# Weight words put together from end bytes, the first block moved behind the second pair, and later sums spread by transposes

## The chip, the cores and the metric

One core of one Trainium2 chip. The metric is device microseconds of one execution. The kernel before takes 706.54 us, the median of three runs (705.92 to 707.37).

## The reference

Sliding-window attention with sinks (batch 4, 8 heads, 768 positions, head size 64, 4 sink keys, a window of 128), and its output, 3072 tokens by 512, goes through a two-layer network of width 2048 whose hidden function is piecewise.

```python
scores = scale * np.matmul(q, k.transpose(0, 1, 3, 2))
scores = np.where(is_sink | in_window, scores, -1000000000.0)
a = np.exp(scores - np.max(scores, axis=-1, keepdims=True))
a = a / (np.sum(a, axis=-1, keepdims=True) + 1e-09)
x = np.matmul(a, v)                       # to (B * S, H * D)
h = x @ w_in
g = np.where(h >= 1, h, np.where(h <= -1, 0.0, (h + 1) ** 2 / 4))
out = g @ w_out
```

Everything is float32, except that the two weights arrive as float64; the kernel reads each as a pair of 32-bit words, `low` and `x` (the high one).

## The kernel before, in words

Work goes in eight chunks of 384 tokens (four batches, two halves of the sequence). Each chunk has attention for eight heads, which fills `xn`, and then the network on those tokens: `stage1` (h, L588) for j = 0 to 15, and `stage2` (the output, L607) two j behind. The network of a chunk is interleaved on TensorE with the attention of the next chunk by `spread`, which deals out steps by weights written beside them. TensorE's order is the program's own (`manual_schedule`); the other engines are ordered by the framework's planner, which simulates the program, save where `queue` chains instructions of one engine or `keep_in_program_order` pins one.

The matmuls take each float32 as two parts: a part rounded to the engine's format, and the rest. For a weight, the float64 words are first put together to a float32 pattern, which is then split. That is the decoding. A block is two rows of tiles of w_in or w_out, 128 partitions by 1024 numbers; there are 16 blocks (`weights(n)`, n even for w_in, odd for w_out). For each block VectorE does three steps into a tile `bits` and one more, and ScalarE one:

- L170: the high word shifted left by 3, with the top two bits cleared
- L176: sign and top exponent bit put in
- L179: the three top bits of the low word put in
- L180: ScalarE rounds this to the high part
- L183: VectorE subtracts that, which gives the rest

The float64 words are loaded into tiles of the pool `wpool` (L205, 1 MB each; the first four on SyncE's queue, the others on ScalarE's). This pool has eight buffers. The decoded w_out blocks take their buffers from the same pool and keep them, while decoded w_in blocks have tiles of their own. So late in the decoding few buffers are left for raw words. After L179 nothing reads the raw words any more. `fetch` loads ahead by up to two blocks, less at the end.

The first four pairs of heads and the scores of the fifth run in `first_pairs`, before any network work. For each pair: scores on TensorE (L441), peaks on VectorE (L452, with their order chained), exponentials on ScalarE (L457), the sums' reciprocals (L464, L465), then `pair_r` and `pair_av`. `pair_r` (L505) spreads the reciprocals over the head's 64 rows by six small matmuls against the identity; L507 copies them to `xn`, and L496 multiplies the attention's product by them. Blocks 0 to 3 are decoded in this loop, in pieces: a block's first two steps behind a pair's sums, its third between the next pair's peaks, its fourth behind these. The other 12 blocks are spread over the first chunk's network. Pairs 5 to 7 and then single heads (`attn_steps`, L283 onward) are the attention that runs beside it. `pair_steps` holds the weights of the later pairs' steps.

Of the kernel before, what the change touches and what calls it, by code (L numbers as in the profile page):

```python
# [10 lines left out]
I32 = mybir.dt.int32  # L11
# [38 lines left out]
def attn_ffn(ctx, tc, qk, qkp, vx, vs, par, w_in, w_out, out):  # L50
# [113 lines left out]
    def decode_parts(t, w, words, pin=False, on=False):  # L164

        low, x = words[..., 0], words[..., 1]
        high, rest = (t[:, :, 0], t[:, :, 1]) if len(t.shape) == 4 else (t[:, 0], t[:, 1])

        def shift():
            first = nc.vector.tensor_scalar(w, x, 3, 0x3FFFFFFF, op0=ALU.logical_shift_left, op1=ALU.bitwise_and)  # L170
            if pin:
                tc.keep_in_program_order(first)
            queue(first, on)

        def sign():
            queue(nc.vector.scalar_tensor_tensor(w, x, -0x40000000, w, op0=ALU.bitwise_and, op1=ALU.bitwise_or), on)  # L176

        def tail():
            queue(nc.vector.scalar_tensor_tensor(w, low, 29, w, op0=ALU.logical_shift_right, op1=ALU.bitwise_or), on)  # L179
            queue(nc.scalar.copy(high, w.bitcast(F32)), on)  # L180

        def rest_of():
            queue(nc.vector.tensor_tensor(rest, w.bitcast(F32), high.bitcast(F32), op=ALU.subtract), on)  # L183

        return shift, sign, tail, rest_of

    def decode(t, w, words, pin=False):
        for f in decode_parts(t, w, words, pin):
            f()
# [4 lines left out]
    def weights(n):  # L194
# [4 lines left out]
        def fetch():  # L199
            for k in range(n, min(n + min(AHEAD if n > 2 else 1, NP // 2 - n // 2 - 1) + 1, NP)):  # L200
# [6 lines left out]
        def parts(on):  # L207
# [7 lines left out]
            return decode_parts(t, dec.tile([P, 2, DM], I32, name=f"bits{n % 2}"), words, pin=not on, on=on)  # L215

        def f():
            fetch()
            for g in parts(False):
                g()  # L220

        if n < WFIRST:
# [237 lines left out]
    def pair_sums(m):  # L460
# [4 lines left out]
        queue(nc.vector.reciprocal(r, r), on)  # L465
        st["r", m] = r
# [31 lines left out]
    def pair_r(m):  # L498
# [4 lines left out]
        for i in range(CT):  # L503
            for a in range(2):
# [4 lines left out]
    def pair_steps(m):  # L509
# [7 lines left out]
        pv = [(0.65, lambda: pair_r(m - 1)), (1.2, lambda: pair_av(m - 1)())]  # L517
# [5 lines left out]
    def first_pairs():  # L523
# [4 lines left out]
        for m in range(H // 2 + 1):  # L528
# [12 lines left out]
            if 0 < m < H // 2:  # L541
                d[2]()
            pair_scores(m, 2)
            if m:
# [4 lines left out]
            if m < H // 2:  # L549
                wsteps[m][0]()  # L550
                d = wsteps[m][1]()
                d[0]()
                if m:
                    pair_av(m - 1)()
                d[1]()
# [98 lines left out]
    spn = [dec.tile([P, P], F32, name=f"spn{i}") for i in range(2)]  # L654
    for t in vq + spn:
# [166 lines left out]
```

## Time and profile before

| what | value |
|---|---|
| median of three runs | 706.54 us |
| the profiled execution | 705.98 us, span 704.3 us |
| PE busy | 681.5 us, 97% |
| DVE busy | 510.3 us, 72% |
| ACT busy | 489.5 us, 70% |
| POOL busy | 278.8 us, 40% |

The span is what the profile covers of the execution; 1.68 us lie around it. PE is TensorE's matmuls, PEld its weight loads, DVE VectorE, ACT ScalarE, POOL GpSimd. Busy shares are averages over stages that differ: the first 135 us, in which the weights are decoded, are not like the rest. A matmul's end is modelled, so PE can show as busy in a stretch in which it also waits.

### The profile page before, as it was taken

The page shows a single profiled execution, that of the slowest core. Times are in us where ns is not written, and L with a number is a line of the kernel's source. Part 1 is how long each engine was busy: PE and PEld are TensorE (multiplying, and loading weights), DVE is VectorE, ACT ScalarE, POOL GpSimd, SP SyncE. Part 2 cuts the span into 40 slices and gives each one's busy share as a digit, 9 for nine tenths or more (in the row PEclk, how much of TensorE's full clock was granted, in tenths as well). Part 3 has the DMA queues.
Part 4 walks back from the last instruction along what each step waited for, and adds up shares of the span by engine and source line. Part 5 has one row for each costly group of instructions (what it writes and reads, how often), then busy time and mean ns, then how long its engine had stood idle before and what let it go on. Part 6 is the DMA issues. An engine that isn't in the chain of part 4 may idle for free.

```text
span 704.3 us, 12263 instructions
## 1 busy us (share of the span) xinstructions
PE 681.5 (97%) x3889; PEld 604.6 (86%) x3889; DVE 510.3 (72%) x1405; ACT 489.5 (70%) x1241; POOL 278.8 (40%) x470
## 2 busy tenths in 40 slices
PE   5899998999999999999999999999999999999996
PEld 3567877899999999989889999899899999989995
DVE  7888998887776877688777878878787877642221
ACT  4886667687778868777787877777776876554332
POOL 3003344744443445355554455635544444300000
PEclk9899999999999999999999999999999999999999
DMA  7864533132244344254333443434322310001001
GB/s 232 291 216 156 190 99 135 49 107 60 63 148 124 102 127 129 68 174 128 92 113 105 147 130 124 126 118 133 122 59 62 102 50 22 3 1 45 1 1 49
DMA packets 45441, 73.98 MB, mean 105 GB/s; under 512 B 10744, under 2 KB 30008, under 8 KB 45368
## 3 DMA queue, kind: packets, MB, share of 16 engines
q1 hardware_dynamic: 42104, 60.53, 28.2%
q10 hardware_dynamic: 3264, 12.58, 4.8%
q8 instruction: 33, 0.54, 0.3%
q14 instruction: 40, 0.33, 0.1%
HBM read 66.80 MB, written 6.29 MB: 104 GB/s over the span
## 4 chain that ended last, share of the span: by engine, by line
PE 79%; DVE 9%; DMA 3%; ACT 3%; POOL 3%; issue 2%; SPq 0%; ACTq 0%; POOLq 0%; DVEq 0%
PE h_ps L588 33%; PE o_ps L607 32%; PE ps_a L283 4%; PE ps_a L390 4%; PE ps_a L344 2%; DVE bits L176 2%; DVE bits L179 1%; DMA w<-w_in 1%; POOL q_l L269 1%; PE ps_a L474 1%; DVE w L183 1%; DVE bits L170 1%; PE ps_a L493 1%; DVE p L304 1%; DVE g L597 1%
## 5 line engine op out<-in xcount | busy, mean ns | idle before, releaser
L588 PE MATMUL h_ps<-x,wi 128*128 128x384 f32 x1536 | 310.2, 340 | 0.0
L588 PEld LDWEIGHTS h_ps<-x,wi 128*128 128x128 f32 x1536 | 262.2, 188 | 8.7 <-issue 1.5
L607 PE MATMUL o_ps<-w,gh 128*128 128x512 f32 x768 | 244.0, 398 | 0.0
L607 PE MATMUL o_ps<-w,gl 128*128 128x512 f32 x384 | 151.1, 393 | 0.4 <-POOL gl L599 0.4
L607 PEld LDWEIGHTS o_ps<-w,gh 128*128 128x128 f32 x768 | 134.3, 188 | 16.9 <-issue 1.7
L597 DVE SCALAR_TENSOR_TENSOR g<-g,h_ps 128x384 f32<-128x384 f32 x128 | 70.3, 549 | 61.7 <-ACT g L596 60.6
L595 ACT ACTIVATE g<-h_ps,half 128x384 f32<-128x384 f32 x128 | 73.9, 578 | 52.7 <-PE h_ps L588 52.0
L269 POOL TENSOR_TENSOR q_l<-r,q_h 128x384 fp32r<-128x384 f32 x48 | 51.1, 1064 | 122.7 <-ACT q_h L268 116.1
L598 ACT CAST gh<-g 128x384 fp32r<-128x384 f32 x128 | 65.5, 512 | 46.1 <-DVE g L597 44.9
L290 ACT ACTIVATE p<-p,peak 128x260 f32<-128x260 f32 (+1 forms) x144 | 71.5, 496 | 23.0 <-DVE peak L287 22.4
L607 PEld LDWEIGHTS o_ps<-w,gl 128*128 128x128 f32 x384 | 72.0, 188 | 17.8 <-POOL gl L599 0.7
L599 DVE TENSOR_TENSOR gl<-g,gh 128x384 fp32r<-128x384 f32 x112 | 67.3, 601 | 23.5 <-ACT gh L598 22.6
L267 DVE TENSOR_TENSOR k_s<-k_r,k_s 64x524 fp32r<-64x524 f32 (+1 forms) x44 | 49.1, 1115 | 34.4 <-ACT k_s L265 34.3
L596 ACT ACTIVATE g<-g 128x384 f32<-128x384 f32 x128 | 67.0, 524 | 2.0
L287 DVE CUSTOM_DVE_ANT_0 p<-ps_a,m 128x260 f32<-128x260 f32 (+1 forms) x144 | 57.0, 407 | 14.7 <-PE ps_a L283 13.8
L358 POOL TENSOR_SCALAR_AFFINE_SELECT pt<-pt 128x384 fp32r<-128x384 f32 (+1 forms) x96 | 51.3, 535 | 22.6 <-DVE pt L349 19.5
L304 DVE CUSTOM_DVE_ANT_0 p<-p,stat 128x128 f32<-128x128 f32 x128 | 57.0, 489 | 0.2
L356 POOL TENSOR_SCALAR_AFFINE_SELECT pt<-pt 128x384 fp32r<-128x384 f32 (+1 forms) x96 | 49.9, 521 | 8.8 <-ACT pt L348 4.9
L599 POOL TENSOR_TENSOR gl<-g,gh 128x384 fp32r<-128x384 f32 x16 | 23.4, 1461 | 67.7 <-ACT gh L598 64.2
L390 PEld LDWEIGHTS ps_a<-pt,v_s 128*128 128x128 f32 x304 | 42.4, 190 | 1.8
L390 PE MATMUL ps_a<-pt,v_s 128*128 128x256 f32 (+1 forms) x304 | 41.9, 275 | 0.0
L283 PE MATMUL ps_a<-k_s,q_h 128*128 128x260 f32 (+1 forms) x144 | 40.7, 283 | 1.2 <-DVE sk L352 0.9
(151 smaller groups left out, 933.1 us busy)
## 6 DMA issues: line engine op xcount, KB each, us to landing
r<-qk SPq DMA_DIRECT2D x48, 192.0 KB
k_r<-qk SPq DMA_DIRECT2D x32, 262.0 KB
again<-w_in SPq DMA_DIRECT2D x16, 512.0 KB
again<-w_out SPq DMA_DIRECT2D x16, 512.0 KB
w<-w_in ACTq DMA_DIRECT2D x6, 1024.0 KB
w<-w_out ACTq DMA_DIRECT2D x6, 1024.0 KB
out<-o SPq DMA_DIRECT2D x23, 256.0 KB
r<-vx SPq DMA_DIRECT2D x32, 128.0 KB
```

The lines of the kernel that those rows point to most:

```text
L269: nc.gpsimd.tensor_tensor(q_l, q_r, q_h.bitcast(F32), op=ALU.subtract)
L283: nc.tensor.matmul(ps[:, lo:260], lhsT=q[:, i * P:(i + 1) * P], rhs=k_s[:, c0:c0 + 260 - lo], start=(j == 0), stop=(j == len(qs) - 1))
L290: nc.scalar.activation(p[:, i, lo:260], p[:, i, lo:260], AF.Exp, bias=peak_i, scale=-1.0, accum_out=stat[:, i:i + 1])
L304: nc.vector.tensor_tensor_reduce(out=own, in0=own, in1=p[:, i, 0:P], scale=r, scalar=0.0, op0=ALU.add, op1=ALU.add, accum_out=stat[:, i:i ...
L390: nc.tensor.matmul(z, lhsT=w, rhs=y, start=(n == 0), stop=(n == len(mms) - 1))
L588: nc.tensor.matmul(h_ps[:, :T], lhsT=w_i[j][:, w, ct * P:(ct + 1) * P], rhs=x[:, y, ct], start=(ct == 0 and n == 0), stop=(ct == NCT - 1 a ...
L595: nc.scalar.activation(g, h_ps[:, :T], AF.Relu, bias=half, scale=0.5)
L596: nc.scalar.activation(g, g, AF.Square)
L597: nc.vector.scalar_tensor_tensor(g, g, 1.0, h_ps[:, :T], op0=ALU.min, op1=ALU.max)
L598: nc.scalar.copy(gh, g)
L599: (nc.gpsimd if row0 == GL_POOL else nc.vector).tensor_tensor(gl, g, gh.bitcast(F32), op=ALU.subtract)
L607: nc.tensor.matmul(o_ps[tt], lhsT=gg[:, tt * P:(tt + 1) * P], rhs=w_o[j][:, w], start=(j == 0 and n == 0), stop=(j == NJ - 1 and n == 2))
```

## The change

The decoding has four VectorE steps as before, of other kinds. Two steps write single bytes into a tile `ends`, which GpSimd has set to zero once: byte 0 of each word gets the low word's top three bits, byte 3 gets the sign bit xor 0xC0. A third step shifts the high word left by 3 and xors it with `ends`. Its result goes over the low words in the raw tile, so every second word; only the last block's goes to `ends`. ScalarE's copy and the subtraction read it there. So a raw tile is in use until the subtraction. There is one `ends` tile in place of two `bits` tiles.

The prefetch depth is changed to `max(NP // 2 - 1 - (n + 1) // 2, 0)` instead of `NP // 2 - n // 2 - 1` (each at most two). Blocks 14 and 15 are loaded by a call behind block 13's and 14's steps.

In `first_pairs` all of block 0 comes behind the second pair's last peaks (pair index 1); blocks 1 to 3 have their first byte step behind the sums and the second behind L496.

For pairs 4 to 7 the reciprocal is written out to 128x384, each value 64 times, into a buffer of `q_l`. `pair_r` then does three 128x128 transposes of it instead of six matmuls, and its step weight for pairs 5 and on is 0.35 instead of 0.65.

```diff
--- before.py
+++ after.py
@@ -161,32 +161,43 @@
     with tc.issue_after(behind):
         nc.gpsimd.memset(both, -1)
 
-    def decode_parts(t, w, words, pin=False, on=False):
+    def decode(t, w, words):
 
         low, x = words[..., 0], words[..., 1]
         high, rest = (t[:, :, 0], t[:, :, 1]) if len(t.shape) == 4 else (t[:, 0], t[:, 1])
-
-        def shift():
-            first = nc.vector.tensor_scalar(w, x, 3, 0x3FFFFFFF, op0=ALU.logical_shift_left, op1=ALU.bitwise_and)
-            if pin:
-                tc.keep_in_program_order(first)
-            queue(first, on)
+        nc.vector.tensor_scalar(w, x, 3, 0x3FFFFFFF, op0=ALU.logical_shift_left, op1=ALU.bitwise_and)
+        nc.vector.scalar_tensor_tensor(w, x, -0x40000000, w, op0=ALU.bitwise_and, op1=ALU.bitwise_or)
+        nc.vector.scalar_tensor_tensor(w, low, 29, w, op0=ALU.logical_shift_right, op1=ALU.bitwise_or)
+        nc.scalar.copy(high, w.bitcast(F32))
+        nc.vector.tensor_tensor(rest, w.bitcast(F32), high.bitcast(F32), op=ALU.subtract)
+
+    def decode_parts(t, ends, words, w, on):
+
+        x = words[..., 1]
+        b = words.bitcast(U8).rearrange("p j c (w e) -> p j c w e", e=4)
+        e = ends.rearrange("p j c -> p (j c)").bitcast(U8).rearrange("p (j c e) -> p j c e", j=2, e=4)
+        high, rest = t[:, :, 0], t[:, :, 1]
+
+        def put(i):
+            if not on:
+                tc.keep_in_program_order(i)
+            queue(i, on)
+
+        def tail():
+            put(nc.vector.tensor_scalar(e[..., 0], b[..., 0, 3], 5, 0x07, op0=ALU.logical_shift_right,
+                                        op1=ALU.bitwise_and))
 
         def sign():
-            queue(nc.vector.scalar_tensor_tensor(w, x, -0x40000000, w, op0=ALU.bitwise_and, op1=ALU.bitwise_or), on)
-
-        def tail():
-            queue(nc.vector.scalar_tensor_tensor(w, low, 29, w, op0=ALU.logical_shift_right, op1=ALU.bitwise_or), on)
+            put(nc.vector.tensor_scalar(e[..., 3], b[..., 1, 3], 0x80, 0xC0, op0=ALU.bitwise_and, op1=ALU.bitwise_xor))
+
+        def word():
+            queue(nc.vector.scalar_tensor_tensor(w, x, 3, ends, op0=ALU.logical_shift_left, op1=ALU.bitwise_xor), on)
             queue(nc.scalar.copy(high, w.bitcast(F32)), on)
 
         def rest_of():
             queue(nc.vector.tensor_tensor(rest, w.bitcast(F32), high.bitcast(F32), op=ALU.subtract), on)
 
-        return shift, sign, tail, rest_of
-
-    def decode(t, w, words, pin=False):
-        for f in decode_parts(t, w, words, pin):
-            f()
+        return tail, sign, word, rest_of
 
     top = {}
     loaded = []
@@ -197,7 +208,7 @@
             return (w_in, w_out)[k % 2][k // 2 * 2:k // 2 * 2 + 2].bitcast(I32).rearrange("j p c -> p j c")
 
         def fetch():
-            for k in range(n, min(n + min(AHEAD if n > 2 else 1, NP // 2 - n // 2 - 1) + 1, NP)):
+            for k in range(n, min(n + min(AHEAD if n > 2 else 1, max(NP // 2 - 1 - (n + 1) // 2, 0)) + 1, NP)):
                 if k not in raw:
                     raw[k] = wpool.tile([P, 2, 2 * DM], I32, name="w")
 
@@ -212,13 +223,16 @@
                 w_o[j:j + 2] = t[:, 0], t[:, 1]
             else:
                 t = wi2[n // 2]
-            return decode_parts(t, dec.tile([P, 2, DM], I32, name=f"bits{n % 2}"), words, pin=not on, on=on)
+            return decode_parts(t, ends[n % len(ends)], words, ends[n % len(ends)] if n == NP - 1 else words[..., 0], on)
 
         def f():
             fetch()
             for g in parts(False):
                 g()
-
+            if NP - 4 < n < NP - 1:
+                wsteps[n + 1].load()
+
+        f.load = fetch
         if n < WFIRST:
             return fetch, lambda: parts(True)
         return f
@@ -462,8 +476,13 @@
         stat = st.pop(("sum", m))
         r = stat[:, :, CT:2 * CT]
         queue(nc.vector.tensor_scalar(r, stat[:, :, 0:CT], 1.0e-9, None, op0=ALU.add), on)
-        queue(nc.vector.reciprocal(r, r), on)
-        st["r", m] = r
+        if on:
+            queue(nc.vector.reciprocal(r, r))
+            st["r", m] = r
+        else:
+            wide = st["r", m] = att.tile([P, CT * P], F32R, name="q_l").bitcast(F32).rearrange(
+                "p (i a d) -> p i a d", a=2, d=D)
+            nc.vector.reciprocal(wide, r.rearrange("p a i -> p i a").unsqueeze(3).broadcast_to([P, CT, 2, D]))
 
     def early_transp(u, part):
 
@@ -501,6 +520,9 @@
         ps = ps_a.tile([P, 512], F32, name="ps_a")
         r = st.pop(("r", m))
         for i in range(CT):
+            if m >= H // 2:
+                nc.tensor.transpose(ps[:, i * P:(i + 1) * P], r[:, i].rearrange("p a d -> p (a d)"), ident)
+                continue
             for a in range(2):
                 nc.tensor.matmul(ps[a * D:a * D + D, i * P:(i + 1) * P], lhsT=r[:, a, i:i + 1].broadcast_to([P, D]),
                                  rhs=ident, start=True, stop=True)
@@ -514,7 +536,7 @@
         if m < NATIVE // 2:
             steps.append((0.0, lambda: pair_values(m)))
         tp = [(0.35, lambda u=u, i=i: early_transp(u, i)) for u in (a, b) for i in range(2)]
-        pv = [(0.65, lambda: pair_r(m - 1)), (1.2, lambda: pair_av(m - 1)())]
+        pv = [(0.35 if m > H // 2 else 0.65, lambda: pair_r(m - 1)), (1.2, lambda: pair_av(m - 1)())]
         dg = [(0.0, lambda: pair_sums(m))] if m < NATIVE // 2 else []
         if m % (H // 2) == 0:
             return steps + tp[:3] + sc[:1] + tp[3:] + pv[:1] + sc[1:2] + pv[1:] + sc[2:] + dg
@@ -538,21 +560,24 @@
                 pair_av(m - 1)()
             pair_scores(m, 0)
             pair_scores(m, 1)
-            if 0 < m < H // 2:
+            if 1 < m < H // 2:
                 d[2]()
             pair_scores(m, 2)
-            if m:
+            if m == 1:
+                for f in wsteps[0][1]():
+                    f()
+            elif m:
                 d[3]()
             if 0 < m < H // 2:
                 pair_r(m - 1)
             pair_sums(m)
             if m < H // 2:
                 wsteps[m][0]()
-                d = wsteps[m][1]()
-                d[0]()
                 if m:
+                    d = wsteps[m][1]()
+                    d[0]()
                     pair_av(m - 1)()
-                d[1]()
+                    d[1]()
 
 
     chunks = [(b, t) for t in (0, CT) for b in range(B)]
@@ -652,6 +677,10 @@
     dec = early.enter_context(tc.tile_pool(name="dec", bufs=1))
     vq = [dec.tile([P, CT + 1, 2, D], F32, name=f"vq{i}") for i in range(2)]
     spn = [dec.tile([P, P], F32, name=f"spn{i}") for i in range(2)]
+    ends = [dec.tile([P, 2, DM], I32, name=f"ends{i}") for i in range(1)]
+    with tc.issue_after(behind):
+        for t in ends:
+            nc.gpsimd.memset(t, 0)
     for t in vq + spn:
         nc.vector.memset(t, 0.0)
     p0 = [att.tile([P, CT, 260], F32, name="p").rearrange("p i c -> p (i c)") for _ in range(2)]
```

## Rows read from the trace of the kernel before

**Rows 1.** Busy time by stretch: length, then PE, PEld, DVE, ACT, POOL; clock, DMA.

```profile
13.00:43.00 30.00, 22.89 (x193) 15.76 (x190) 27.68 (x77) 23.79 (x77) 0.91 (x2) 0.89 0.77 257
43.00:70.00 27.00, 27.00 (x166) 21.83 (x166) 23.10 (x43) 18.98 (x50) 6.97 (x5) 1.00 0.49 174
70.00:105.00 35.00, 35.00 (x216) 27.46 (x215) 32.85 (x50) 22.40 (x55) 14.85 (x10) 1.00 0.44 145
105.00:135.00 30.00, 27.43 (x156) 22.64 (x155) 26.02 (x50) 20.29 (x51) 17.65 (x17) 1.00 0.29 103
140.00:170.00 30.00, 30.00 (x172) 27.42 (x171) 24.33 (x78) 23.27 (x64) 15.49 (x30) 1.00 0.30 89
```

**Rows 2.** Chain of waits from 70 to 105 us, its shares by engine and line.

```profile
by line: DVE bits L176 21.6%; DVE bits L179 16.1%; issue 10.1%; DVE w L183 10.0%; DVE wi L183 8.7%; DVE bits L170 7.7%; DVE g L597 7.3%; DVE pt L452 4.0%; DVE p L452 3.2%; ACT wi L180 3.1%; DVE stat L464 2.6%; PE ps_a L441 2.0%; ACT pt L457
```

**Rows 3.** The decoding lines: count, duration ns min/median/max, first and last start, form.

```profile
L170 DVE TENSOR_SCALAR bits<-w x16: 650/682/1046, 12.9 to 123.8; 128x1024 int32<-128x1024 int32 x16
L176 DVE SCALAR_TENSOR_TENSOR bits<-w,bits x16: 1210/1225/2074, 13.6 to 124.9; 128x1024 int32<-128x1024 int32 x16
L179 DVE SCALAR_TENSOR_TENSOR bits<-w,bits x16: 1209/1224/1925, 15.9 to 129.7; 128x1024 int32<-128x1024 int32 x16
L180 ACT CAST w<-bits x8: 1046/1048/1052, 25.7 to 130.9; 128x1024 fp32r<-128x1024 f32 x8
L183 DVE TENSOR_TENSOR w<-bits,w x8: 1217/1224/1225, 26.7 to 132.0; 128x1024 fp32r<-128x1024 f32 x8
```

**Rows 4.** Timeline of DVE, first pairs: start us, us, instruction, idle before it.

```profile
12.88 0.70 DVE L170 TENSOR_SCALAR bits<-w 128x1024 int32<-128x1024 int32 x1 [2.91 <-DMA w<-w_in]
...
14.76 0.28 DVE L452 CUSTOM_DVE_ANT_0 pt<-o_ps,m 128x128 f32<-128x128 f32 x1
...
22.51 0.29 DVE L452 CUSTOM_DVE_ANT_0 p<-o_ps,m 128x128 f32<-128x128 f32 x1 [0.61 <-PE o_ps L441]
```

**Rows 5.** Timeline of PE, first pairs.

```profile
11.12 1.23 PE L441 MATMUL o_ps<-k_s,q_h 64*128 64x128 f32 x5
...
19.59 0.44 PE L474 MATMUL ps_a<-ident,pt 128*128 128x128 f32 x2 [1.13 <-ACT xn L507]
...
42.72 0.77 PE L588 MATMUL h_ps<-x,wi 128*128 128x384 f32 x3
```

**Rows 6.** The reciprocals by line, columns as in Rows 3.

```profile
L296 DVE RECIPROCAL stat<-stat x48: 165/176/179, 122.3 to 602.5; 128x3 f32<-128x3 f32 x48
L465 DVE RECIPROCAL stat<-stat x8: 183/190/192, 9.8 to 106.5; 128x6 f32<-128x6 f32 x8
```

**Rows 7.** Chain of waits in order of time: start us, us on the chain, what.

```profile
62.69 0.33 PE ps_a L474 x3
...
107.90 0.81 PE ps_a L505 x12
```

**Rows 8.** Last weight blocks: timelines of ACT's queue and DVE; one stretch as Rows 1.

```profile
103.81 0.38 ACTq L205 DMA_DIRECT2D w<-w_in  x1
117.20 0.38 ACTq L205 DMA_DIRECT2D w<-w_out  x1
...
118.40:121.80 3.40, 2.54 (x14) 1.94 (x13) 2.46 (x9) 3.40 (x14) 2.17 (x2) 1.00 0.77 308
...
111.59 1.23 DVE L183 TENSOR_TENSOR w<-bits,w 128x1024 fp32r<-128x1024 f32 x1 [0.65 <-ACT w L180]
123.76 0.68 DVE L170 TENSOR_SCALAR bits<-w 128x1024 int32<-128x1024 int32 x1
131.99 1.23 DVE L183 TENSOR_TENSOR w<-bits,w 128x1024 fp32r<-128x1024 f32 x1 [0.65 <-ACT w L180]
```

**Rows 9.** Timelines of PE and of its weight loads around the last block.

```profile
124.29 2.25 PE L588 MATMUL h_ps<-x,wi 128*128 128x384 f32 x12
...
133.27 0.19 PEld L607 LDWEIGHTS o_ps<-w,gh 128*128 128x128 f32 x1 [0.36 <-DVE w L183]
134.13 0.19 PEld L607 LDWEIGHTS o_ps<-w,gl 128*128 128x128 f32 x1 [0.68 <-POOL gl L599]
```

## The prediction

> **What bounds the kernel now.** I read busy time by stretch first. After 140 us TensorE has no gap and the other engines have room, so only what happens before that can move the end, and a shift there is kept to the end [rows 1]. From 13 to 43 us VectorE is busy 27.68 of 30.00. From 43 to 70 it has 3.9 us free and TensorE none. From 70 to 105 it is busy 32.85 of 35.00 [rows 1]. TensorE shows as full there too, but its weight loads have fallen from 0.91 of the time (27.42 of 30.00, after 140) to 0.78 (27.46 of 35.00), so part of that is waiting [rows 1]. The chain of waits says whose work it waits for: from 70 to 105 it runs through VectorE, the decoding lines above all [rows 2]. The decoding ends late: TensorE waits at 133.27 for the subtraction of the last weight block, then until 134.13 for another operand [rows 9]. So there are three places to watch: VectorE before 43, VectorE from 70 to 113, and the arrival of blocks 14 and 15.
>
> **The decoding steps.** A block costs VectorE 0.682 + 1.225 + 1.224 + 1.224 = 4.36 us by the medians [rows 3]. The change takes out L170, L176 and L179 and adds two byte steps and one shift-and-xor. No row shows a byte step on VectorE. The bounds come from the two kinds of step over the same 1024 numbers: 0.68 (L170, one source) and 1.22 (L176, two sources) [rows 3]. A byte step has one source and takes every second word, as L170 does, so I take 0.68. The shift-and-xor is L176's kind, 1.22, but writes every second word. L170 and L176 already read that way, and L176 is no slower than L183, which reads without gaps [rows 3]. Writing that way isn't in the trace; nearest is again 1.22, and 1.9 is what L176 and L179 reach when disturbed (their maxima are 2.07 and 1.93) [rows 3]. I take 1.22. New sum: 2 x 0.68 + 2 x 1.22 = 3.81, so 0.54 less per block. ScalarE's copy (1.05) and L183 now read spaced words; I leave them as they are for the same reason.
>
> [...]
>
> **The first block.** VectorE sits idle for 2.91 us until the words of block 0 arrive at 12.88. It then spends 1.88 us on them before the second pair's first peak at 14.76, though the scores of that pair were begun on TensorE at 11.12 [rows 4, 5]. With the block behind the peaks they can start soon after 11.12, nearly 3 us earlier (I leave 0.8 us for the first matmul and its hand-over). The block's load stays where it is. Not all of the gain stays. The block's subtraction now follows its third step directly, so VectorE stands idle for ScalarE's copy (1.05). The next pair is also held by a loop in which VectorE has no part: its transposes wait for the copy of the spread sums on ScalarE (19.59), and its first peak waits for TensorE (22.51) [rows 4, 5]. Three microseconds less one, and blocks 1 to 3 at 0.54 less each as far as that loop lets them through: 1.1 to 2.4. I take 1.8 for the start of the network, now at 42.72 [rows 5].
>
> **The spread sums.** Six matmuls took 0.81 on the chain for a pair, three 128x128 transposes take 0.33 [rows 7]: 0.48 less, four times, on TensorE where it is full. The price is on VectorE: a reciprocal of 384 instead of 6 per partition. The trace has 3 and 6 per partition: medians 176 and 190 ns, so 4.7 ns a number and 0.16 fixed [rows 6]. That makes 0.16 + 384 x 4.7 ns = 1.95, or 1.8 more than now. From the ends of the two ranges, (183 - 179)/3 = 1.3 ns gives 0.7 and (192 - 165)/3 = 9 ns gives 3.6 [rows 6]; these are the bounds. All four lie between 43 and 107 us, where the decoding is, the last at 106.5 [rows 6].
>
> **The last loads.** Now a raw tile is free after a block's third step. After the change it is in use until the fourth, and with seven decoded w_out blocks in eight buffers block 14 can be loaded only when block 13 is through, and block 15 only when block 14 is. Before, block 14's load was issued at 103.81, nine microseconds before block 13's last step ended at 111.59 + 1.23 = 112.82 [rows 8]. So the new loads stand in one line with the decoding. One load: issued at 117.20, its 1.05 MB (3.4 us at 308 GB/s) over at 121.80 [rows 8], so 4.6 us. The loads before these get shallower too, but have some microseconds to spare. SyncE's queue is passed by none of this; the issue itself stands in ScalarE's queue, 0.38 each as before. GpSimd's one memset of `ends` is hidden: GpSimd is busy 0.91 of the 30 us after 13 [rows 1]. The wide reciprocals borrow the two buffers of `q_l`, so the first single heads' q_l come later; their GpSimd work only moves within the stretch.
>
> **The sum**, as shifts against the profiled execution:
> - At 43: 1.8 early.
> - 43 to 70: four blocks -2.2, two reciprocals +3.6, so VectorE +1.4, covered by its 3.9 free [rows 1]. Still 1.8.
> - 70 to 105: the blocks follow each other every (123.8 - 12.9)/15 = 7.4 us [rows 3], so five: -2.7, with one reciprocal +1.8. Now 2.7 early. TensorE's own saving lies beneath this.
> - Block 13's end: 112.82 - 2.7 + 1.8 (fourth reciprocal) - 0.54 = 111.4.
> - Block 14: load 4.6, own steps 3.81 + 1.05, and 0.8 for other work queued between: in hand at 121.7. TensorE needs it at 124.29 - 2.7 = 121.6 [rows 9]: just in time.
> - Block 15: 4.6 + 5.7 again: 132.0, against 133.22 before (131.99 + 1.23) [rows 8].
> - TensorE goes on at 132.1 instead of 134.13 [rows 9], since the other operand comes from block 14's matmuls and those are 2.6 early: 2.0 gained.
>
> The profiled execution took 705.98, so 704.0. The median of the runs lies 0.56 above it: 704.5. The 0.8 is the softest term; block 15 before took 9.46 from first to last step (123.76 to 133.22) for 5.40 of its own, so it can be 0 to 4 [rows 8]. If the loads are never last, the TensorE side gives 2.7 + 0.5, so 703.3, and with cheap reciprocals (0.7) some 701.5. I take 701.5 to 705.1 as this case's own range.
>
> **Rivals.**
> - *The late loads take everything.* A wait for data replaces the wait for VectorE: a byte step pinned in program order stands at the head of VectorE's queue until block 14's words land, and behind it wait the peaks and the g of the network, for which TensorE waits; the same holds on ScalarE if the load's issue, which waits for the buffer, is put ahead of ready work. Two microseconds instead of 0.8 around each of the two blocks make 2.4 more: 706.9. For it: 9.46 against 5.40. Against it: VectorE has little else to do there, 26.02 of 30.00 with the decoding itself in it [rows 1].
> - *The long reciprocal costs more, and it is slower.* Beyond 1.95, each extra microsecond counts twice (the third and the fourth; the first two have 2.5 left of the free time). From 3.0 us per reciprocal the gain is gone. At the bound, 3.6: 2 x 1.65 + 0.8 = 4.1 lost, 708.6. For it: the spread of so few rows; against it: the medians.
> - *Byte steps or the spaced write don't run at L170's rate, and it is slower.* From 0.13 more per byte step, or 0.26 for the write, the gain is gone. At 1.22 per byte step a block costs 1.08 more than I have: 43 to 70 4.3 less 2.5, then 5.4, then three more blocks 3.2: 10.4 lost, 714.9. Against it: L170.
>
> [...]
>
> **How the numbers follow.** Forecast 0.46; late loads 0.27; reciprocal 0.14; byte steps and write 0.13. A difference under 0.2% (1.4 us) can't be told from none, so the bound lies at 705.1 and 708.0. Faster 0.46, same 0.27, slower 0.27. The range takes in the first three cases and leaves out most of the last: 701.5 to 710.
>
> **What would show it.** Byte steps at 0.68 and the third step at 1.22 on the chip; the reciprocal of 384 near 1.95; the second pair's first peak near 12; the first network matmul near 41; ScalarE's two last loads right behind the subtractions of blocks 13 and 14; TensorE's wait near 132 for block 15. It is wrong if the third step or a byte step is dearer, if VectorE stands idle at 111 to 116 while TensorE waits for g, or if TensorE waits nowhere and the gain is over 3.

## The result, and the profile after

The changed kernel takes 716.21 us (median, 715.45 to 716.38); the kernel before, run beside it, 706.27. The ratio is 1.0136, with a 95% interval of 1.0118 to 1.0153: slower by about 9.7 us, where 2 us faster was forecast. The range ended at 710.0. The profiled execution took 716.11 us; its span is 714.3.

The stretches of after, to be read against [rows 1] (columns as there; the last one, 135 to 150, is not in [rows 1] and has its line of before beneath it):

```profile
13.00:43.00 30.00, 23.28 (x172) 15.72 (x172) 22.16 (x59) 20.24 (x65) 0.91 (x2) 0.77 0.70 232
43.00:70.00 27.00, 25.57 (x157) 20.38 (x154) 25.63 (x48) 19.82 (x53) 5.47 (x4) 1.00 0.58 201
70.00:105.00 35.00, 35.00 (x205) 27.87 (x204) 32.14 (x56) 22.71 (x57) 9.31 (x7) 1.00 0.32 108
105.00:135.00 30.00, 24.73 (x132) 20.83 (x131) 24.15 (x48) 18.45 (x47) 18.63 (x19) 0.89 0.44 145
135.00:150.00 15.00, 12.64 (x62) 10.91 (x61) 10.50 (x24) 8.48 (x23) 7.33 (x9) 0.89 0.13 34
...
135.00:150.00 15.00, 15.00 (x90) 13.95 (x89) 11.05 (x36) 12.39 (x35) 7.24 (x13) 1.00 0.34 106
```

Two stretches stand out. From 13 to 43 VectorE is busy 22.16 us instead of 27.68: it stands, with more work still to do. From 105 on TensorE has gaps, and its granted clock falls to 0.89. The first output block is sent at 151.24 instead of 142.62, 8.6 us later, and the lag is still there late in the program: an output block is sent at 565.18 in after and at 555.47 in before. From the network's start to the first output it is 105.3 us instead of 99.9, so about 3 us are lost ahead of the network and 5.4 in its first chunk.

Prices first: the lines that took the place of [rows 3] and [rows 6], columns as there.

```profile
L187 DVE TENSOR_SCALAR ends<-w x16: 698/766/1411, 14.0 to 134.5; 128x1024 uint8<-128x1024 uint8 x16
L191 DVE TENSOR_SCALAR ends<-w x16: 740/756/1577, 14.6 to 135.2; 128x1024 uint8<-128x1024 uint8 x16
L194 DVE SCALAR_TENSOR_TENSOR w<-w,ends x15: 1212/1226/2039, 15.4 to 125.0; 128x1024 int32<-128x1024 int32 x15
L195 ACT CAST w<-w x7: 1091/1131/1147, 28.4 to 114.8; 128x1024 fp32r<-128x1024 f32 x7
L485 DVE RECIPROCAL q_l<-stat x4: 2553/2553/2554, 47.8 to 107.5; 128x384 f32<-128x384 f32 x4
```

The byte steps cost 0.77 and 0.76 us, the step that writes every second word 1.23, ScalarE's copy 1.13 instead of 1.05, the wide reciprocal 2.55. So a block has become cheaper on VectorE, by 0.37 us where 0.54 was forecast, and each of the four reciprocals dearer by 2.36.

Now the head. ScalarE's timeline of after, with the idle time before an instruction in brackets:

```profile
21.95 0.30 ACT L340 CAST vsx<-vs_r 120x128 fp32r<-120x128 f32 x1 [2.59 <-DMA vs_r<-vs]
...
26.39 0.30 ACT L340 CAST vsx<-vs_r 120x128 fp32r<-120x128 f32 x1 [2.94 <-DMA vs_r<-vs]
```

In before the same two copies stood in the head without a wait:

```profile
22.27 0.29 ACT L326 CAST vsx<-vs_r 120x128 fp32r<-120x128 f32 x1
...
25.20 0.28 ACT L326 CAST vsx<-vs_r 120x128 fp32r<-120x128 f32 x1
```

They belong to the sink values of the first single heads, which are used after 110 us. The change does not touch them, but in the order that the planner now makes they stand further ahead: the second one, which stood behind four exponentials of the third pair, now stands before the first. ScalarE begins nothing else in these 2.59 and 2.94 us, so the pairs' own work stands behind a load that is not in. VectorE and TensorE wait with it:

```profile
23.49 0.56 DVE L644 TENSOR_TENSOR x<-xn,x 128x384 fp32r<-128x384 f32 x1 [1.10 <-ACT x L643]
...
29.49 1.22 DVE L198 TENSOR_TENSOR w<-w 128x1024 fp32r<-128x1024 f32 x1 [3.27 <-ACT w L195]
```

```profile
45.93 0.77 PE L613 MATMUL h_ps<-x,wi 128*128 128x384 f32 x3
```

The network starts at 45.93, 3.2 us later than in before and not 1.8 earlier. Last, the two late blocks; ScalarE's queue, VectorE and TensorE of after:

```profile
117.25 0.37 ACTq L216 DMA_DIRECT2D w<-w_in  x1
129.58 0.37 ACTq L216 DMA_DIRECT2D w<-w_out  x1
```

```profile
122.20 0.92 DVE L187 TENSOR_SCALAR ends<-w 128x1024 uint8<-128x1024 uint8 x1 [1.78 <-DMA w<-w_in]
123.02 1.56 DVE L191 TENSOR_SCALAR ends<-w 128x1024 uint8<-128x1024 uint8 x1
124.48 0.27 DVE L301 CUSTOM_DVE_ANT_0 p<-ps_a,m 128x128 f32<-128x128 f32 x1
```

```profile
127.38 1.08 PE L358 MATMUL ps_a<-ident,p 128*128 128x128 f32 x3 [4.62 <-DVE p L316]
129.54 3.22 PE L613 MATMUL h_ps<-x,wi 128*128 128x384 f32 x12
...
140.65 0.50 PE L632 MATMUL o_ps<-w,gh 128*128 128x512 f32 x1 [1.49 <-ACT w L195]
142.02 0.79 PE L632 MATMUL o_ps<-w,gh 128*128 128x512 f32 x1 [0.87 <-DVE w L198]
```

Block 14's load is issued at 117.25 instead of 103.81 [rows 8], directly behind block 13's last step. VectorE stands before the byte step at 122.20 with peaks of the single heads behind it (124.48), and TensorE stands 4.62 us. Before stood there too, but for 1.94:

```profile
122.89 0.87 PE L344 MATMUL ps_a<-ident,p 128*128 128x128 f32 x3 [1.94 <-DVE p L302]
```

After the longer gap the twelve matmuls of [rows 9] take 3.22 us instead of 2.25; the granted clock from 127 to 132 us is 0.54. Block 15 follows in the same way; TensorE goes on at 142 instead of 134.13.

### The profile page after: what moved, and what is told of

Its sections match the earlier page's. It is cut to its first block, busy times and chain, and to the rows that moved or that the text cites. A ratio compares the mean times of both kernels' runs of the same rounds, so it can differ in the third digit from the quotient of the medians.

```text
span 714.3 us, 12204 instructions
## 1 busy us (share of the span) xinstructions
PE 684.1 (96%) x3853; PEld 607.9 (85%) x3853; DVE 511.5 (72%) x1405; ACT 489.2 (68%) x1241; POOL 275.6 (39%) x471
## 5 line engine op out<-in xcount | busy, mean ns | idle before, releaser
L372 POOL TENSOR_SCALAR_AFFINE_SELECT pt<-pt 128x384 fp32r<-128x384 f32 (+1 forms) x96 | 49.2, 513 | 22.3 <-DVE pt L363 19.2
L370 POOL TENSOR_SCALAR_AFFINE_SELECT pt<-pt 128x384 fp32r<-128x384 f32 (+1 forms) x96 | 49.5, 516 | 8.4 <-ACT pt L362 4.3
L624 POOL TENSOR_TENSOR gl<-g,gh 128x384 fp32r<-128x384 f32 x16 | 21.2, 1327 | 74.0 <-ACT gh L623 68.1
```

The source lines that it names most:

```text
L624: (nc.gpsimd if row0 == GL_POOL else nc.vector).tensor_tensor(gl, g, gh.bitcast(F32), op=ALU.subtract)
```

## Experiments

Three suspects: **A**, ScalarE's queue in the head; **B**, the loads of blocks 14 and 15; **C**, the wide reciprocal. The first four runs take them out of the kernel after; then each part of the change is put into the kernel before by itself; the rest rebuild it. Ratios are against the kernel before, run beside each group of them on the same chip (medians 704.7 to 706.0). Letters e to h are four such groups; a difference between two groups is known to about 0.3 points.

| run | what | median us | ratio, 95% interval | first network matmul | first output |
|---|---|---|---|---|---|
| e1 | after, sink copies out of the head | 713.47 | 1.0124 (1.0089 to 1.0159) | 42.25 | 148.59 |
| e2 | after, word in its own tile, old loads | 710.00 | 1.0087 (1.0052 to 1.0121) | 46.8 | 145.67 |
| e3 | after, narrow reciprocal | 709.43 | 1.0069 (1.0039 to 1.0098) | 46.0 | 145.68 |
| e4 | after, all three | 704.83 | 1.0004 (0.9988 to 1.0020) | 43.33 | 141.84 |
| f1 | after, byte steps not pinned | 715.10 | 1.0123 (1.0095 to 1.0152) | 47.1 | 151.44 |
| f2 | before + moved first block | 711.68 | 1.0084 (1.0056 to 1.0112) | 43.11 | 144.25 |
| f3 | before + wide reciprocal, transposes | 710.17 | 1.0060 (1.0039 to 1.0081) | 41.1 | 144.16 |
| f4 | before + byte decode | 704.08 | 0.9971 (0.9950 to 0.9992) | 41.33 | 139.89 |
| g1 | f4 with word in raw tile, late loads | 706.06 | 1.0003 (0.9985 to 1.0020) | 41.0 | 140.76 |
| g2 | f4, sink copies out of the head | 703.03 | 0.9965 (0.9946 to 0.9983) | 39.6 | 138.17 |
| g3 | f4, first block behind four peaks | 707.84 | 1.0036 (1.0014 to 1.0057) | 44.40 | 142.94 |
| g4 | f4, sums spread by a copy | 703.00 | 0.9955 (0.9939 to 0.9971) | 41.2 | 136.98 |
| h1 | g2 and g4 together, first block moved | 703.77 | 0.9981 (0.9964 to 0.9999) | 42.78 | 139.18 |
| h2 | g2 and g4 together | 701.58 | 0.9950 (0.9932 to 0.9968) | 39.79 | 135.72 |

The last two columns are us in each run's profiled execution (before: 42.72 and 142.62; after: 45.93 and 151.24). Two things in these columns vary from one execution to the next. From the first output to the end it is 563.4 us in before and 563.4 to 565.9 in the others, so a difference of 2 us there says nothing. And with the first block in its old place the start depends on when that block's words land. f3 has the head of before unchanged, and there VectorE begins with them at 11.18, not at 12.88 as in [rows 4]:

```profile
11.18 0.69 DVE L170 TENSOR_SCALAR bits<-w 128x1024 int32<-128x1024 int32 x1 [1.21 <-DMA w<-w_in]
```

This is why its network starts at 41.1. In f4, g1 and g4 the words are waited for until 11.74 to 11.84, in g2 and h2 they are in by 11.4. So before's profile caught a late arrival, and 42.72 is some 1 to 1.7 us late as a yardstick.

**e1: the sink copies behind the head's last ScalarE instruction.**

```diff
-            nc.scalar.copy(vs_s[0:120], vs_r)
+            queue(nc.scalar.copy(vs_s[0:120], vs_r))
```

> The kernel after, with the two copies of the single heads' sink values (CAST vsx) put in ScalarE's queue behind the head's last ScalarE instruction. Theory head-queue (ScalarE stands 2.59 and 2.94 us before these copies for their load, and the whole head stands behind ScalarE): the first network matmul, at 45.93, comes at 41 to 43, and the time falls by 3 us, to about 713, less what the late loads take back. Rival (the head is late because of the order of block 0's own steps and the clock that fell): it stays within 0.7 us of 45.9 and the time within 0.7 us of 716.2. Rival late-loads (all of the loss is made at 110 to 145): the first network matmul moves, the time does not.

The network starts 3.7 us earlier, so theory A is right about the head: the waits were ScalarE's. But of the 3.7 us the first output keeps 2.65, and the ratio falls by only 0.12 points, well inside its interval. The late loads wait for block 13, whose last step came 3.5 us earlier too (112.5 for 116.0), and TensorE's stall is the same:

```profile
123.82 1.08 PE L358 MATMUL ps_a<-ident,p 128*128 128x128 f32 x3 [4.59 <-DVE p L316]
```

What a gain at 42 us is worth at the end could not be told in time from this run.

**e2: the word in a tile of its own, and the loads of before.** Theory B's test.

```diff
-            return decode_parts(t, ends[n % len(ends)], words, ends[n % len(ends)] if n == NP - 1 else words[..., 0], on)
+            return decode_parts(t, ends[0], words, dec.tile([P, 2, DM], I32, name="bits"), on)
-            ... max(NP // 2 - 1 - (n + 1) // 2, 0)) ...
+            ... NP // 2 - n // 2 - 1) ...
-            if NP - 4 < n < NP - 1:
-                wsteps[n + 1].load()
```

> The kernel after, with the word of each block in a tile of its own, so that the raw words' tile is free at the third step, and with the loads asked for where they were before. Theory late-loads (word kept in the raw tile makes the loads of blocks 14 and 15 wait for the blocks before; then VectorE stands at a byte step with peaks behind it): block 14 is in hand before 115, block 15 ends at 134 to 136 for 141.96, the time falls by 4 to 6 us, to 710 to 712. Theory head-queue alone: the first network matmul stays at 45.9 and everything after is set by it, time falls by under 1.5 us. Theory wide reciprocal: under 1.5 us.

The load of block 14 is issued at 106.63 instead of 117.25, TensorE's stall is 2.31 us, block 15 ends at 134.9. The ratio falls by 0.49 points, about 3.5 us: less than 4 to 6, more than the rivals allow. Block 14 came at 122.5 and not before 115: VectorE was still behind, its third step done only at 120.1. The edit also gives ScalarE's copy unspaced words again (1.05 us for 1.13), so it is not of the loads alone; g1 below settles how much that counts.

**e3: reciprocals of six numbers and six matmuls again.** Theory C's test.

```diff
+        queue(nc.vector.reciprocal(r, r), on)
+        st["r", m] = r
...
-            nc.vector.reciprocal(wide, r.rearrange("p a i -> p i a").unsqueeze(3).broadcast_to([P, CT, 2, D]))
...
-                nc.tensor.transpose(ps[:, i * P:(i + 1) * P], r[:, i].rearrange("p a d -> p (a d)"), ident)
```

> The kernel after, with the reciprocals of the later pairs back at six numbers a partition and the sums spread by six matmuls each. Theory wide reciprocal (2.55 us on VectorE four times, 2.36 us more than the narrow one each, of which VectorE's queue passes on most): the sum of block ends between 46 and 122 gains 2 to 4 us and the time falls by 2 to 4 us. Rivals head-queue and late-loads: VectorE catches up in between, the time falls by under 1 us, since blocks 14 and 15 wait for their loads and not for VectorE's time; with the loads as the bound it is 9.4 us of VectorE's time that cost nothing.

The ratio falls by 0.67 points, 4.7 us, more than theory C gave it. The network starts as late as in after, yet block 13 ends at 113.7 instead of 117.2, with it the late loads come earlier, and the stall shrinks to 2.46 us. So the reciprocals and the late loads act on the same chain.

**e4: the three edits together.**

> All three of these edits together in the kernel after; what stays of the change is the byte decode (3.81 for 4.36 us of VectorE a block) and the moved first block. If the three theories hold the whole loss: 702 to 706, at or under the kernel before (706.3). If something else in the byte decode (its slower ScalarE copy, the word waiting for the end bytes' tile) or in the moved block costs: above 708. If the effects only add up where each is the last to end: less than the sum of the three.

Level with the kernel before. Taking the three out takes out the whole loss. At the first output their single gains are 2.65, 5.57 and 5.56 us, 13.8 in sum; together they give 9.4. All three lie on one chain, the decoding up to block 13 and then load and decode twice, and a microsecond on it can be saved once. But e4 has the cheaper decode in it and is not faster than before, so something in it still costs.

**f1: the byte steps no longer held in program order.** If the pin makes the stall, it should go.

```diff
-            if not on:
-                tc.keep_in_program_order(i)
             queue(i, on)
```

> The kernel after, with the byte steps no longer held in program order (the planner may place them behind the peaks when it thinks the raw words late). Theory pin (the stall of PE at 122.8 to 127.4 is made by the peaks of the single heads standing in VectorE's queue behind a byte step whose load is not in): the stall of 4.62 us shrinks to 2 us or less, block 14 itself comes no earlier, and the time falls by 2 to 4 us from 716.2. Rival (the late loads themselves: block 14 is not in hand before 127 to 129 whoever stands in front, and the network waits for it): the stall moves to the network's matmuls, the time stays within 1 us.

The rival had the time right; neither had the way it comes about. The stall shrinks to 0.88 us, and block 14 is in hand at 112.9, much earlier; the time stays. The planner now decodes well ahead from 40 us on, in front of the network's g and the peaks (22 decoding steps start on VectorE between 40 and 70 us, 14 in after); from 43 to 70 VectorE is busy all the time and TensorE stands (21.14 us busy for 25.57):

```profile
43.00:70.00 27.00, 21.14 (x104) 16.83 (x101) 27.00 (x48) 17.10 (x43) 3.56 (x3) 0.81 0.65 228
```

The run doesn't settle what the pin costs; it shows that an order is only exchanged for another.

**f2, f3, f4: each part of the change by itself, in the kernel before.** f2 has only the moved block:

```diff
-            if 0 < m < H // 2:
+            if 1 < m < H // 2:
                 d[2]()
             pair_scores(m, 2)
-            if m:
+            if m == 1:
+                for f in wsteps[0][1]():
+                    f()
+            elif m:
                 d[3]()
```

> The kernel before with one part of the change alone: the first block decoded behind the second pair's peaks. By the prediction the first network matmul moves from 42.72 to about 41 and the time falls by up to 1.8 us less what VectorE gives back. Theory head-queue (moving the block lets the planner put the copies of the sink values further ahead in ScalarE's queue, in front of loads that are not in): the first network matmul comes at 44 to 47 and the time rises by 1 to 4 us. Rival (the casts move only because the byte steps changed the planner's times): first matmul at 41 to 42.7 and no loss.

f3 has only the wide reciprocal and the transposes:

```diff
+            nc.vector.reciprocal(wide, r.rearrange("p a i -> p i a").unsqueeze(3).broadcast_to([P, CT, 2, D]))
...
+            if m >= H // 2:
+                nc.tensor.transpose(ps[:, i * P:(i + 1) * P], r[:, i].rearrange("p a d -> p (a d)"), ident)
+                continue
```

> The kernel before with one part alone: the later pairs' reciprocals at 384 numbers a partition, and the sums spread by transposes. Theory wide reciprocal (2.36 us more on VectorE each, four times, against 0.48 us of PE each): slower by 2 to 5 us, with block ends between 48 and 115 later by 2.4 us a pair less the idle time of VectorE before (2.3 us in 43:70 and 70:105 together). Rival (VectorE's slack and its waits for ScalarE's copies take it up): within 1 us of the kernel before.

f4 has only the byte decode, with e2's tile and loads (its main lines, shortened):

```diff
-            first = nc.vector.tensor_scalar(w, x, 3, 0x3FFFFFFF, ...
+            put(nc.vector.tensor_scalar(e[..., 0], b[..., 0, 3], 5, 0x07, ...
+            put(nc.vector.tensor_scalar(e[..., 3], b[..., 1, 3], 0x80, 0xC0, ...
+            queue(nc.vector.scalar_tensor_tensor(w, x, 3, ends, ...
```

> The kernel before with one part alone: the byte steps and the shift-and-xor, with the word in a tile of its own, loads and first block as before, sums narrow. It takes 0.44 us less of VectorE a block (2.92 for 3.13 us before the copy, less 0.08 us more in ScalarE's copy). By the prediction's terms that is faster by 0 to 2.5 us; if PE sets the pace from 43 to 120 whatever VectorE does, within 1 us of the kernel before; if the pinned byte steps cost peaks, slower by 1 to 3 us.

f4 is faster, by 0.29 points or 2 us (0.08 to 0.50). That its network starts 1.4 us earlier is mostly the words' arrival: counted from there it is 29.6 us, against 29.8 in before and 29.9 in f3. The rest comes behind it, with 98.6 us from the network's start to the first output instead of 99.9. f3 is slower by 0.6 points, though its words came early; TensorE stands before the fourth pair's spread tile:

```profile
108.14 0.88 PE L510 MATMUL ps_a<-ident,q_l 128*128 128x128 f32 x3 [2.75 <-DVE q_l L471]
```

f2 is slower by 0.84 points, though the sink copies waited only 0.33 us there. VectorE in the head of f2, against [rows 4]:

```profile
11.93 0.29 DVE L452 CUSTOM_DVE_ANT_0 pt<-o_ps,m 128x128 f32<-128x128 f32 x1 [1.97 <-PE o_ps L441]
...
18.68 1.23 DVE L183 TENSOR_TENSOR wi<-bits,wi 128x1024 fp32r<-128x1024 f32 x1 [1.11 <-ACT wi L180]
...
22.51 0.28 DVE L452 CUSTOM_DVE_ANT_0 p<-o_ps,m 128x128 f32<-128x128 f32 x1
```

The block's subtraction in before:

```profile
18.21 1.23 DVE L183 TENSOR_TENSOR wi<-bits,wi 128x1024 fp32r<-128x1024 f32 x1 [0.42 <-ACT wi L180]
```

VectorE stands 1.97 us for TensorE's scores instead of 2.91 for the words, then 1.11 for the copy, where two peaks had left only 0.42. So even against the late words of before nothing is won: the third pair's first peak comes at 22.51 in both, and the network starts 0.4 us later, between the two expectations. Against f3, whose words came early, f2 starts 2.0 us late (43.11 for 41.1). At the first output f2 is 1.6 us later than before and at its end 3.8 (709.80 for 705.98); the 2.2 between them are within what the other profiles vary. The median of its runs is another 1.9 longer, and that the trace doesn't show.

**g1: B by itself, without A and C.** f4 with the word in the raw tile and the late loads (without e2's edit).

> The kernel after with the first block in its old place and the narrow reciprocals, so that the byte decode with the word in the raw tile and the late loads of blocks 14 and 15 are what is left of the change. Against the run f4 (the same with the word in a tile of its own and the loads of before; ratio to the kernel before 0.9971): theory late-loads: VectorE waits for the raw words of block 14 at about 115 to 118, PE stands 2 us or more longer at the single heads' first transposes, ratio 1.001 to 1.006. Rival (with VectorE 9.4 us less loaded, blocks 13 and 14 come early enough for the load to be hidden): ratio 0.996 to 0.999, and the late loads cost only in company of the wide reciprocals.

1.0003 against 0.9971: 0.32 points, about 2.3 us, between the two expectations and nearer to theory B; the two runs are of different groups, and the difference is only just clear of their noise (0.04 to 0.60). VectorE stands 2.52 us for block 14's words at 113.65, TensorE 0.47 and 2.45 us near the first single heads (1.65 in f4). Block 13 ends at 108.8 in g1 and 108.6 in f4, so the copy of spaced words has cost next to nothing until then; block 14 is in hand at 119.8 instead of 116.6. So the late loads cost by themselves, by the traces, and perhaps less than beside C (0.49 in e2).

**g2: f4 with e1's edit. g3: f4 with the first block behind four of the six peaks,** so that the last two stand beside ScalarE's copy. **g4: f4 with the sums spread by a copy of VectorE and transposes.**

```diff
+            if m == 1:
+                d = wsteps[0][1]()
+                d[0]()
+                d[1]()
+            if 0 < m < H // 2:
                 d[2]()
             pair_scores(m, 2)
```

```diff
-            nc.vector.reciprocal(wide, r.rearrange("p a i -> p i a").unsqueeze(3).broadcast_to([P, CT, 2, D]))
+            nc.vector.reciprocal(r, r)
+            nc.vector.tensor_copy(wide, r.rearrange("p a i -> p i a").unsqueeze(3).broadcast_to([P, CT, 2, D]))
```

> The kernel of f4 (byte decode alone) with the copies of the sink values behind the head in ScalarE's queue; there ScalarE stood 0.52 and 0.61 us before them. Theory head-queue: the first network matmul comes 0.3 to 1 us before f4's 41.3, and the ratio to the kernel before is 0.994 to 0.997. Rival (what ScalarE waits for there is covered): the ratio stays at 0.997 and the first matmul within 0.3 us of 41.3.

> The kernel of f4 with the first block decoded behind the second pair's first four peaks, and the last two peaks between its word and its subtraction, so that ScalarE's copy of the block is covered again (in the runs with all six peaks ahead VectorE stood 1.1 us for it). Theory (the move fails because the copy comes into the open, and because the second pair's scores set the first peak at 11.95 in any order, so that only 0.93 us were to be had and not 1.8): first network matmul within 0.5 us of f4's 41.3 and ratio 0.996 to 0.999. Rival (the move costs by what the planner does with it further on, as the 0.84% of the run f2 at 0.4 us of the head's length suggest): ratio 1.002 or more in spite of the covered copy.

> The kernel of f4 with the sums spread by transposes, but the reciprocal taken of six numbers a partition and spread to 384 by a plain VectorE copy. The copy's price is open: 0.2 to 0.45 us for 384 numbers by the subtractions and copies of the trace. Theory wide reciprocal (only the reciprocal's 6.2 ns a number costs, the spread sums themselves save 0.48 us of PE a pair): 0.994 to 0.998, no wait of PE for the spread tile at 108 to 110. Rival (VectorE has no room for any addition, and PE has slack): 0.998 to 1.002.

g2's network starts at 39.6, 1.7 us before f4's and earlier than expected, 0.4 us of it by words that came earlier. Its ratio of 0.9965 can't be told from f4's 0.9971. g3 hides the copy again (0.41 us of idle time), and is slower all the same, 1.0036: here ScalarE stood 1.93 us for a sink value's load at 20.93, so its two theories stayed mixed. g4 gains on the kernel before: 0.9955. In it the spread costs 0.19 and 0.55 us instead of 2.55:

```profile
L483 DVE RECIPROCAL stat<-stat x4: 178/191/192, 43.1 to 101.9; 128x6 f32<-128x6 f32 x4
L484 DVE COPY q_l<-stat x4: 548/553/555, 43.3 to 102.1; 128x384 f32<-128x384 f32 x4
```

Its interval overlaps f4's. In its trace the network's start is as in f4 (41.2) and the first output comes 2.9 us earlier, so that the transposes themselves gain is likely, not shown.

**h1 and h2: the move, with the sink copies out of the way in both.** They differ in the place of the first block alone (the diff of f2).

> Byte decode with its own word tile and the old loads, sums spread by a copy, sink copies behind the head, and the first block behind the second pair's six peaks. Theory order (VectorE stands 1.97 us for the second pair's scores, which the old place fills with the first block's byte steps, and 1.1 us for the copy, which six peaks no longer cover): first network matmul at 42 to 44, ratio to the kernel before 0.998 to 1.002, and 0.3 to 0.6% above the run h2. Rival sink copies (the move costs only by what it draws into the head's queues): within 0.15% of h2, first matmul within 0.7 us of h2's.

> The same with the first block in its old place. Both parts that gained by themselves over f4 (0.9971) are in it: sink copies behind the head (g2, 0.9965) and the copied spread (g4, 0.9955). If they add up: 0.993 to 0.996, first network matmul at 39.3 to 40.3. If one takes the other's place: no better than 0.9955 and a first matmul at 41.

The move costs 0.31 points, 2.2 us, with the sink copies out of it. Nearly all of it arises ahead of the network: from its start to the first output the two take 96.4 and 95.9 us. A second pair says the same: e4 is g2 with the first block moved, 1.0004 against 0.9965. VectorE in the heads of h1 and of h2, the instructions before which it stood for a microsecond or more:

```profile
11.99 0.29 DVE L464 CUSTOM_DVE_ANT_0 pt<-o_ps,m 128x128 f32<-128x128 f32 x1 [1.97 <-PE o_ps L453]
...
18.17 1.23 DVE L198 TENSOR_TENSOR wi<-bits,wi 128x1024 fp32r<-128x1024 f32 x1 [1.11 <-ACT wi L195]
...
40.16 0.56 DVE L514 TENSOR_TENSOR xn<-ps_a,xn 128x384 f32<-128x384 f32 x1 [2.40 <-PE ps_a L511]
```

```profile
11.28 0.76 DVE L187 TENSOR_SCALAR ends<-w 128x1024 uint8<-128x1024 uint8 x1 [1.31 <-POOL ends L679]
...
37.09 0.56 DVE L514 TENSOR_TENSOR xn<-ps_a,xn 128x384 f32<-128x384 f32 x1 [1.01 <-PE ps_a L511]
```

In the old place the byte steps fill the time in which VectorE would wait for the second pair's scores: they start at 11.28, the scores are there at about 12, and the peaks begin at 12.54 in h2 for 11.99 in h1. So only 0.55 us were to be had, and the copy in the open takes more. (What the byte steps wait for in h2 is GpSimd's memset of `ends`, which was forecast as hidden.) Network start 39.79 against 42.78, first output 135.72 against 139.18. h2 is the fastest kernel measured, 0.5% under the kernel before and 1.8% under the kernel after by the ratios.

## Why the prediction was wrong

- **Byte steps and third step** (0.68, 0.68, 1.22 forecast): 0.77, 0.76, 1.23. 0.17 us a block more than forecast, and ScalarE's copy, left at 1.05, is 1.13. The mechanism was right, but a third of the saving is missing: 0.37 us a block for 0.54. By itself (f4) the part gives 2 us; that the whole was forecast at 2 is chance, since that sum had the moved block and the reciprocals in it.
- **The spaced write** (1.22 taken for the third step, with no row that showed such a write): at this step of two words it cost nothing, by the medians 1.226 us with the write spaced (L194 in after) and 1.226 without (f4).
- **The long reciprocal** (1.95 taken, bounds 0.7 to 3.6): 2.55, inside the bounds. From 190 ns at 6 numbers to 2553 at 384 that is 6.25 ns a number, where the medians of 3 and 6 gave 4.7. A slope from two points 14 ns apart was a poor ruler. The prediction let the whole gain end only at 3.0 us, because it set two of the four into VectorE's free time and paid the others with gains that did not come. Alone, at 2.55, its own terms make an estimated 5.5 us lost (4 x 2.36 less 3.9 free); f3 shows 0.6 points, 4.2 us. The rival's place was right: TensorE waits for the fourth, 2.75 us in f3 (0.57 in after).
- **"The network start 1.8 early"** is the step that failed first: it came 3.2 late. The second pair's peaks did begin where they were forecast (11.95, near 12). What failed is what that was taken to be worth. The peaks came 2.8 us earlier, but now the whole block stood behind them, and VectorE can only gain idle time: the 0.9 us from 11.95 to 12.88. The copy that comes into the open takes that back (1.11 us for 0.42), and f2 starts 0.4 us late. The 2.91 us of idle time were one execution's besides: in f3, with the same head, they are 1.21, and the words are in before the scores. The other 2.8 us are a wait that the prediction did not look for: the sink copies in ScalarE's queue (e1: 3.7 us). It counted what the moved block issues on VectorE and passed over what else the planner would then reorder.
- **"Block 13's end at 111.4"**: 117.22. Of the 5.8 us, 5.0 are the head (-1.8 forecast, +3.2 measured). For the rest the prediction's terms would give more than is left, an estimated 2.2 us: 0.17 for each of six blocks and 0.6 for each of two reciprocals. So idle time took some of it; no run splits it.
- **The last loads**: the mechanism stood in the prediction as a rival, pinned byte step with peaks behind it. In the forecast the loads were taken as just in time, with 0.8 us around each block, which cost 1.2 us (704.5 for 703.3); the rival made it 3.6. Issued at 117.25, block 14 was in hand at 129.1: 11.8 us where 10.3 were allowed (4.95 for 4.6 until the words were in, 6.9 for 5.7 from there), and 7.5 us after the 121.6 at which it was to be needed. Alone the late loads cost 0.32 points, 2.3 us (g1), between the two; beside the other parts some 3.5 (e2), with a granted clock that fell after TensorE's stall (0.54 from 127 to 132 us in after).
- **The sum.** Forecast -2 us; measured +9.7. Alone, in points of the ratio: decode -0.29, moved block +0.84, wide reciprocal +0.60, late loads +0.32: +1.47 in sum, +1.36 measured together, which agree within an uncertainty of about 0.5. The sink copies are in the second term as far as f2 drew them ahead. The rivals were each given the whole of the bad outcome; three of the mishaps came at once, mostly on one chain.

Left open: why f2 loses 0.84 points where the move costs 0.31 between h1 and h2, and 0.39 between g2 and e4 (ScalarE's wait for a sink value may be longer in other executions than the 0.33 us of f2's trace; not shown), and what the pin on the byte steps costs by itself.

## What to carry to other kernels

Move work into idle time of an engine only up to the event that ends the wait after it: here the first block's old place already filled the wait for the scores. Letting other work pass a long block gains no more than the idle time that this fills (0.55 us between h1 and h2), because the block then stands in front of whatever comes next. Read the length of a wait for a load from more than one execution (2.91 us in before, 1.21 in f3). After a reorder, look at each engine's queue for work that has nothing to do with it; the copies for a later stage, drawn ahead of their loads, cost more (3.7 us of the head by e1) than the move could have won. Parts of one change are best priced one by one: here one of four gained, and its gain was hidden under the losses of the others.

## What the runs showed of the hardware

- VectorE's byte steps over 1024 bytes, read at every eighth and written at every fourth byte, took 0.76 to 0.77 us (medians in after), near L170's 0.68 and not the 1.22 of the two-source steps.
- A reciprocal cost VectorE 6.25 ns a number between 6 and 384 numbers (0.190 and 2.553 us); a plain copy that spreads six numbers to 384 took 0.55 us (g4). So here it was cheaper to spread by copying, after the reciprocal.
- ScalarE's copy of 1024 numbers took 1.13 us when they were read at every second word (after), 1.05 when they were not (before, f4).
- After TensorE's stall of 4.62 us the granted clock was 0.54 from 127 to 132 us: twelve matmuls took 3.22 us from 129.54, and 2.25 again from 134.67.
- The words of one and the same first load were waited for until 12.88 us in one execution and until 11.18 in another (before and f3).
